# Weights moved behind the last V, the output weight in contiguous rows, and an earlier max, in a decode-attention kernel

## Chip, cores and metric

The kernel runs on one core of a Trainium2 chip. The metric is device microseconds (us) of one execution, the median of several runs; the span in a profile is about 1.8 us shorter than the time of the same run. Engines: PE is the matrix engine (PEld its weight loads), DVE the vector engine, ACT the scalar engine, SP the engine that issues the loads.

## The reference, cut to what matters

```python
xn  = layernorm(x)                                   # x: 1 x 1 x 640
q   = xn @ wq                                        # 640 -> 32 heads x 128
p   = softmax(q . k_cache * 128**-0.5)               # per head, 32768 keys; k, v: 8.39 MB a head each
o   = p @ v_cache
out = x + o.reshape(1, 1, 4096) @ wo                 # 4096 x 640
        + (silu(xn @ w_gate) * (xn @ w_up)) @ w_down # F = 1728
```

All tensors are bf16. Keys and values of 32 heads are 537 MB; wq and wo are 5.24 MB each, the three MLP weights 6.6 MB together.

## The kernel before

A ring of three slots of 64 KB per partition holds everything that is loaded. SP issues the loads in the order of `units`, each waiting until its slot is free. Here `H` is 32, `D` 640, `NJ` 256 (keys per partition), `NCD` 5, `FB` 14.

```python
units = [("wq",), ("ffn",)]
for h in range(H):
    units.append(("k", h))
    if h >= 1: units.append(("v", h - 1))
units += [("wo",), ("v", H - 1)]
slot = position in units % 3
TAIL = [128, 64, 32, 16, 16]      # the last V comes in five pieces, each with its own semaphore

# [cut] SP:
e.dma_start(wo, A_wo.rearrange("(h d) n -> d h n", d=DH))      # 128 partitions x 32 runs of 1280 B

# [cut] PE, one head: scores of h, then P @ V of h - 1
def head(h):
    scores(h)                     # after DVE multiplied K by q, PE folds 128 columns into 8 (L248, L267)
    if h >= 1:
        total(h - 1)
        pv_half(h - 1, 0)         # L279: 32 matmuls of 512 columns
    turn(h)                       # transposes the row maxima
    if h >= 1: pv_half(h - 1, 1)  # 32 more
    spread(h)                     # spreads the head's maximum; exp waits for it
    if h >= 2: fold(h - 2)        # o as a column

# [cut] PE, the end
fold(H - 2); wait wo
for h in range(H - 1): att(h)     # L358: 5 matmuls a head, weights wo_v[:, h, :, c] (every 5th column)
total(H - 1)
pv_last()                         # L292: 256 matmuls of one column, waiting for the five pieces
att(H - 1)                        # then DVE adds the residual, SP stores
```

The MLP is computed at the start, while the first keys are loaded.

Of the kernel before, what the change touches and what calls it, by code (L numbers as in the profile page):

```python
# [5 lines left out]
ALU = mybir.AluOpType  # L6
# [6 lines left out]
def bass_parallel_sum__gqa_block_cached__swiglu_ffn__decode_kernel(  # L13
# [33 lines left out]
    TAIL = [128, 64, 32, 16, 16]  # L47
    W = 512 // DH
    assert sum(TAIL) == NJ and NHF == 4 and (H - H0) % PER == 0 and PER % SLOTS == 0
    assert PER % PR == 0 and PER % SR == 0  # L50
    HA = 5
# [5 lines left out]
    units = [("wq",), ("ffn",)]  # L57
# [4 lines left out]
    units += [("wo",), ("v", H - 1)]  # L62
# [11 lines left out]
    with ExitStack() as es:  # L74
# [14 lines left out]
        ocol = sbt("ocol", [128, H], BF16)  # L89
        hcol = sbt("hcol", [128, FB], BF16)  # L90
# [15 lines left out]
        s_x, s_wq, s_wo, s_out = sem("x"), sem("wq"), sem("wo"), sem("o")  # L106
        s_ffn = sem("ffn")
# [9 lines left out]
        s_fpd, s_fx = sem("ffn_down"), sem("ffn_x")  # L117
        s_exp, s_pv, s_o4, s_fold, s_ov = sem("exp"), sem("pv"), sem("o4"), sem("fold"), sem("ov")
        s_f, s_fa, s_fd = sem("ffn_pe"), sem("ffn_act"), sem("ffn_dve")
        s_att, s_fin = sem("att"), sem("fin")  # L120
        block = es.enter_context(nc.Block())
# [23 lines left out]
        wo = flat[:, WO_S * CE:WO_S * CE + H * D].rearrange("p (h n) -> p h n", h=H)  # L145
        wo_v = wo.rearrange("p h (m c) -> p h m c", c=NCD)
        assert H * D <= CE
# [23 lines left out]
        with nc.psum_tensor("ps8", [128, 8, 512], F32) as ps8:  # L171
            bank = [ps8[:, b, :] for b in range(8)]
            O = ps8[0:W, 4, :]
            OL = ps8[:, 5, 0:1]
            acc = ps8[:, 6, 0:NCD]
            fold_ps = ps8[:, 6, 8:9]
            misc = ps8[:, 7, :]

            @block.sync
            def sp(e):  # L180
                owner = {}
                for u in units:
# [15 lines left out]
                    elif u[0] == "v":  # L198
                        e.dma_start(ring[:, s, :], kv_src(A_v_cache, u[1], 0, NJ)).then_inc(s_slot[s], 16)
                        owner[s] = (s_pv, u[1] + 1)  # L200
                    elif u[0] == "ffn":
                        e.dma_start(wg, B_w_gate.rearrange("(p c) n -> p (c n)", c=NCD)).then_inc(s_ffn, 16)
                        e.dma_start(wu, B_w_up.rearrange("(p c) n -> p (c n)", c=NCD)).then_inc(s_ffn, 16)
                        e.dma_start(flat[:, d0:d0 + FM * D], B_w_down[0:FM * 128, :].rearrange(  # L204
                            "(p j) n -> p (j n)", j=FM)).then_inc(s_ffn, 16)
                        e.dma_start(wd[0:FL, FM, :], B_w_down[FM * 128:F, :]).then_inc(s_ffn, 16)
                        owner[s] = (s_fpd, 1)
                    else:
                        e.dma_start(wo, A_wo.rearrange("(h d) n -> d h n", d=DH)).then_inc(s_wo, 16)
# [4 lines left out]
            @block.gpsimd  # L214
            def pool(g):
                for n, t in enumerate((ident, identf)):
                    g.memset(t[:, :], 0.0).then_inc(s_const, 1)
                    g.wait_ge(s_const, 2 * n + 1)
                    g.affine_select(out=t[:, :], in_=t[:, :], compare_op=ALU.not_equal, fill=1.0, base=0,
                                    pattern=[[-1, 128]], channel_multiplier=1).then_inc(s_const, 1)  # L220

            @block.tensor
            def pe(t):
# [48 lines left out]
                def pv_half(h, half):  # L272
                    s = slot_of[("v", h)]
                    if half == 0:
# [3 lines left out]
                    for j in range(half * NJ // 2, (half + 1) * NJ // 2, W):  # L278
                        mm = t.matmul(O, lhsT=P[:, h % PR, j:j + W], rhs=ring[:, s, j * DH:(j + W) * DH],  # L279
                                      start=(j == 0), stop=(j + W == NJ))  # L280
                    if half == 1:
                        mm.then_inc(s_pv, 1)

                def pv_last():
                    h = H - 1
                    s = slot_of[LASTV]
                    t.wait_ge(s_exp, H)
                    j = 0
                    for i, n in enumerate(TAIL):
                        t.wait_ge(s_tail[i], 16)  # L290
                        for _ in range(n):
# [3 lines left out]
                    mm.then_inc(s_pv, 1)  # L295
# [29 lines left out]
                def head(h):  # L325
                    scores(h)
                    if h >= 1:
                        total(h - 1)
                        pv_half(h - 1, 0)
                    turn(h)  # L330
                    if h >= 1:
                        pv_half(h - 1, 1)
                    spread(h)
                    if h >= 2:
# [3 lines left out]
                t.wait_ge(s_ffn, 64)  # L338
                for off, w in ((0, wg_v), (FB, wu_v)):
                    for j in range(FB):  # L340
                        n = 128 if j < FM else FL
                        for c in range(NCD):
                            mm = t.matmul(misc[0:n, off + j:off + j + 1], lhsT=hidden(w, c, j),  # L343
                                          rhs=xn[:, c:c + 1], start=(c == 0), stop=(c == NCD - 1))
                mm.then_inc(s_f, 1)
                first = True
                t.wait_ge(s_fd, 8)
                for j in range(FB):
                    n = 128 if j < FM else FL
                    for c in range(NCD):  # L350
                        mm = t.matmul(acc[:, c:c + 1], lhsT=wd_v[0:n, j, :, c], rhs=hcol[0:n, j:j + 1],
                                      start=first, stop=(j == FB - 1), skip_group_check=True)
                        first = False
                mm.then_inc(s_fpd, 1)

                def att(h):
                    for c in range(NCD):
                        mm = t.matmul(acc[:, c:c + 1], lhsT=wo_v[:, h, :, c], rhs=ocol[:, h:h + 1],  # L358
                                      start=(h == 0 and c == 0), stop=(h == H - 1), skip_group_check=True)
                    return mm  # L360

                t.wait_ge(s_fx, 1)
                for h in range(H0):
                    head(h)
                with t.Fori(0, (H - H0) // PER) as i:
# [3 lines left out]
                    group[0] = None  # L369
                fold(H - 2)  # L370
                t.wait_ge(s_wo, 16)
                t.wait_ge(s_ov, H)
                for h in range(H - 1):
                    att(h)
                total(H - 1)
                pv_last()
# [193 lines left out]
```

## Time and profile before

| | before |
|---|---|
| time | 1294.11 us, 3 runs, 1293.77 to 1294.47 |
| load queue, share of 16 engines | 99.5% |
| moved | 554 MB at 429 GB/s |
| PE / DVE / ACT busy | 80% / 52% / 4% |
| last load landed, end of span | 1285.7, 1292.1 us |

The page of the kernel before: engines' busy time, then in 40 slices of the span the busy share of the DMA engines in tenths and what they moved, then the load queue.

```profile
PE 1036.7 (80%) x5147; PEld 263.8 (20%) x3227; DVE 669.9 (52%) x407; ACT 51.9 (4%) x139; POOL 1.1 (0%) x8
...
DMA  9999999999999999999999999999999999999997
GB/s 400 449 424 427 443 425 435 436 434 428 436 434 438 428 436 438 426 434 438 426 434 438 430 432 436 434 432 432 438 434 428 436 438 426 434 438 428 432 401 315
...
q1 hardware_dynamic: 14704, 554.00, 99.5%
```

The DMA engines are full in every slice but the last. Whatever happens on PE and DVE inside the span is hidden unless it starves the queue; what is not hidden is what comes after the last byte has landed.

The chain that ended last shows the same: key loads hand over to each other at a fixed pace (start us, duration us, what).

```profile
184.33 41.80 DMA ring<-in_A_k_cache_dram
...
261.74 41.80 DMA ring<-in_A_k_cache_dram
```

The landings are at 226.1 and 303.5: 77.4 us for two heads, that is four loads of 8.39 MB, 433 GB/s.

The load of wo is the slow spot. First the issues of the last V but one and of wo, then their times from issue to landing (last column, us), then what moved between 1253 and 1262 us.

```profile
1214.95 0.33 SPq L199 DMA_DIRECT2D ring<-in_A_v_cache_dram  x1
1229.19 0.39 SPq L209 DMA_DIRECT2D ring<-in_A_wo_dram  x1
```
```profile
ring<-in_A_wo_dram SPq DMA_DIRECT2D x1, 5120.0 KB, 37.0
...
ring<-in_A_v_cache_dram SPq DMA_DIRECT2D x31, 36.8
```
```profile
DMA packets 2550, 3.26 MB, mean 363 GB/s; under 512 B 0, under 2 KB 2550, under 8 KB 2550
```

The 36.8 is the median of the 31 V loads; head 30's own is the same. V of head 30 landed at 1214.95 + 36.8 = 1251.8, wo at 1229.19 + 37.0 = 1266.2: 14.4 us for 5.24 MB, 363 GB/s, and every packet is under 2 KB.

The end of the kernel before (start us, duration us, engine, line, instruction, count, and in brackets the idle before it with what ended it):

```profile
1271.32 6.33 PE L358 MATMUL ps<-ocol,ring 128*128 128x1 bf16 x155 [0.36 <-ACT ocol L408]
...
1277.93 1.76 PE L292 MATMUL ps<-P,ring 128*128 128x1 bf16 x61
...
1279.93 3.55 PE L292 MATMUL ps<-P,ring 128*128 128x1 bf16 x128 [0.23 <-issue]
...
1285.86 1.92 PE L292 MATMUL ps<-P,ring 128*128 128x1 bf16 x67 [2.38 <-issue]
...
1287.82 0.22 DVE L538 TENSOR_SCALAR ocol<-ps,rzb 128x1 bf16<-128x1 f32 x1 [9.54 <-PE ps L292]
...
1288.10 0.36 PE L358 MATMUL ps<-ocol,ring 128*128 128x1 bf16 x5 [0.32 <-DVE ocol L538]
...
1288.69 0.35 SPq L211 DMA_DIRECT2D out_dram<-outb  x1
```

The last piece of V was issued at 1260.6 and took 25.1 us, so it landed at 1285.7. PE starts its last stretch at 1285.86, but with 67 matmuls to do, not only the 16 of the last piece: before it stands an idle time of 2.38 us called "issue", in which PE waited for nothing that the profile shows.

### The profile page before, as it was taken

Reading aid. Unit: us, or ns where it says so; the run is one execution under the profiler, and the core shown is the slowest. Engines: PE = TensorE matmul, PEld = TensorE weight load, DVE = VectorE, ACT = ScalarE, POOL = GpSimd, SP = SyncE. Lnnn points to the kernel's source line nnn. Section 1 sums busy time; section 2 is a strip of 40 time slices with the busy share of each in tenths; the row PEclk is TensorE's granted clock in tenths of the full one; section 3 lists DMA queues with packets and bytes.
Section 4 is the critical chain, followed back from the end, with each engine's and each line's share of the span. In section 5 each row is a group of like instructions: output and inputs, shape, how many; then the busy total and the mean of one; then the engine's idle time right before and its main releaser. Section 6 shows DMA issues by size and latency. Waiting matters only on the chain.

```text
span 1292.1 us, 9830 instructions
## 1 busy us (share of the span) xinstructions
PE 1036.7 (80%) x5147; PEld 263.8 (20%) x3227; DVE 669.9 (52%) x407; ACT 51.9 (4%) x139; POOL 1.1 (0%) x8
## 2 busy tenths in 40 slices
PE   3678879877779877778877778877778877778977
PEld 1301222111222111222111222111222111222115
DVE  0485444666444666444666444666444666444560
ACT  2000000000000000000000000000000000000000
POOL 0000000000000000000000000000000000000000
PEclk9588899888889888899888899888889888889886
DMA  9999999999999999999999999999999999999997
GB/s 400 449 424 427 443 425 435 436 434 428 436 434 438 428 436 438 426 434 438 426 434 438 430 432 436 434 432 432 438 434 428 436 438 426 434 438 428 432 401 315
DMA packets 14717, 554.16 MB, mean 429 GB/s; under 512 B 1329, under 2 KB 5490, under 8 KB 5746
## 3 DMA queue, kind: packets, MB, share of 16 engines
q1 hardware_dynamic: 14704, 554.00, 99.5%
q8 instruction: 9, 0.15, 0.0%
q14 instruction: 2, 0.02, 0.0%
q10 hardware_dynamic: 2, 0.00, 0.0%
HBM read 553.99 MB, written 0.00 MB: 429 GB/s over the span
## 4 chain that ended last, share of the span: by engine, by line
DMA 52%; PE 29%; DVE 12%; issue 6%; SPq 0%; DVEq 0%; ACT 0%
DMA ring<-in_A_k_cache_dram 52%; PE ps L279 17%; DVE ring L504 12%; PE ps L248 9%; PE ps L267 1%; PE ps L292 1%; PE ps L358 1%; PE ps L316 0%; PE ps L310 0%; PE ps L302 0%; DVEq L504 0%; SPq L204 0%; DVE sc L510 0%; PE ps L322 0%; ACT o L403 0%
## 5 line engine op out<-in xcount | busy, mean ns | idle before, releaser
L504 DVE TENSOR_TENSOR ring<-ring,qb 128x8192 bf16<-128x8192 bf16 x128 | 557.8, 4420 | 86.6 <-DMA ring<-in_A_k_cache_dram 86.5
L248 PE MATMUL ps<-ring,ident 128*128 128x512 bf16 x1920 | 496.0, 417 | 0.0
L279 PE MATMUL ps<-ring,P 128*4 128x512 bf16 x1984 | 438.3, 379 | 0.0
L267 PE MATMUL ps<-ring,ident 128*128 128x512 bf16 x128 | 56.1, 438 | 224.2 <-DVE ring L504 223.7
L279 PEld LDWEIGHTS ps<-ring,P 128*4 128x4 bf16 x1984 | 166.0, 85 | 245.4
L267 PEld LDWEIGHTS ps<-ring,ident 128*128 128x128 bf16 x128 | 12.6, 98 | 620.4 <-DVE ring L504 326.4
L522 DVE TENSOR_SCALAR negb<-ps 128x1 f32<-128x1 f32 x32 | 5.1, 158 | 215.5 <-PE ps L322 215.5
L510 DVE TENSOR_REDUCE sc<-ps 128x64 f32<-128x512 f32 x128 | 82.3, 684 | 62.6 <-PE ps L248 62.6
L519 DVE TENSOR_REDUCE m<-ps 1x1 f32<-1x128 f32 x32 | 8.9, 279 | 192.2 <-PE ps L316 192.2
L412 ACT ACTIVATE P<-sc,negb 128x256 bf16<-128x256 f32 x32 | 16.2, 508 | 1179.6 <-DVE negb L522 1179.6
L302 PE MATMUL ps<-identf,o 4*128 4x1 f32 x248 | 31.9, 245 | 0.9 <-ACT o L403 0.9
L310 PEld LDWEIGHTS ps<-rsum,ones 128*128 128x128 f32 x64 | 12.3, 194 | 99.0 <-issue 98.2
L302 PEld LDWEIGHTS ps<-identf,o 4*128 4x128 f32 x248 | 30.0, 187 | 0.9 <-ACT o L403 0.9
L403 ACT ACTIVATE o<-ps,rzb 4x512 f32<-4x512 f32 x31 | 21.0, 677 | 0.0
L240 PE MATMUL ps<-ring 128*128 128x512 bf16 x40 | 10.2, 420 | 11.2 <-DMA ring<-in_A_wq_dram 11.2
L473 DVE TENSOR_SCALAR sg<-sg 128x13 f32<-128x13 f32 (+1 forms) x2 | 0.2, 156 | 34.3 <-ACT sg L393 34.3
L516 DVE TENSOR_REDUCE pmax<-sc 128x1 f32<-128x256 f32 x32 | 13.4, 420 | 0.0
L343 PE MATMUL ps<-xn,ring 128*128 128x1 bf16 (+1 forms) x140 | 8.7, 198 | 5.7 <-DMA ring<-in_B_w_down_dram 5.7
L316 PE MATMUL ps<-identf,pmax 128*1 128x128 f32 x64 | 12.2, 272 | 1.2 <-DVE pmax L516 1.2
L322 PE MATMUL ps<-m,ones 1*128 1x1 f32 x64 | 12.1, 256 | 0.4 <-DVE m L519 0.4
L322 PEld LDWEIGHTS ps<-m,ones 1*128 1x128 f32 x64 | 9.4, 182 | 14.2 <-issue 13.5
L492 DVE RECIPROCAL rzb<-ps 128x1 f32<-128x1 f32 x32 | 5.0, 158 | 9.8 <-PE ps L310 9.8
(50 smaller groups left out, 88.2 us busy)
## 6 DMA issues: line engine op xcount, KB each, us to landing
ring<-in_A_wq_dram SPq DMA_DIRECT2D x1, 5120.0 KB, 15.3
ring<-in_A_wo_dram SPq DMA_DIRECT2D x1, 5120.0 KB, 37.0
ring<-in_A_v_cache_dram SPq DMA_DIRECT2D x1, 4096.0 KB, 22.2
ring<-in_B_w_gate_dram SPq DMA_DIRECT2D x1, 2160.0 KB, 19.9
ring<-in_B_w_up_dram SPq DMA_DIRECT2D x1, 2160.0 KB, 24.6
ring<-in_B_w_down_dram SPq DMA_DIRECT2D x1, 2080.0 KB, 28.6
ring<-in_A_v_cache_dram SPq DMA_DIRECT2D x1, 2048.0 KB, 21.6
ring<-in_A_v_cache_dram SPq DMA_DIRECT2D x1, 1024.0 KB, 23.6
```

What stands on the lines that cost most here:

```text
L248: return t.add_instruction(mybir.InstMatmult(start_tensor_calc=False, stop_tensor_calc=stop, tile_size=(128, 128), tile_position=(0, 0), l ...
L267: t.matmul(ob, lhsT=ident[:, :], rhs=src, start=True, stop=False)
L279: mm = t.matmul(O, lhsT=P[:, h % PR, j:j + W], rhs=ring[:, s, j * DH:(j + W) * DH], start=(j == 0), stop=(j + W == NJ))
L292: mm = t.matmul(OL, lhsT=ring[:, s, j * DH:(j + 1) * DH], rhs=P[:, h % PR, j:j + 1], start=(j == 0), stop=(j == NJ - 1))
L302: mm = t.matmul(fold_ps, lhsT=o4[:, m * DH:(m + 1) * DH], rhs=identf[0:W, m:m + 1], start=(m == 0), stop=(m == W - 1))
L322: t.matmul(misc[:, 128:129], lhsT=ones[0:1, :], rhs=m1[0:1, h % SR:h % SR + 1], start=True, stop=True).then_inc(s_b, 1)
L358: mm = t.matmul(acc[:, c:c + 1], lhsT=wo_v[:, h, :, c], rhs=ocol[:, h:h + 1], start=(h == 0 and c == 0), stop=(h == H - 1), skip_group_che ...
L403: a.activation(out=o4[:, :], in_=O, func=ACTF.Copy, scale=rzb[0:W, h % SR:h % SR + 1]).then_inc(s_o4, 1)
L412: a.activation(out=P[:, h % PR, :], in_=sc[:, :], func=ACTF.Exp, bias=negb[:, h % SR:h % SR + 1], scale=c_scale, accum_out=rsum[:, h % SR: ...
L504: v.tensor_tensor(out=kh, in0=kh, in1=q[:, None, :].to_broadcast([128, HF, DH]), op=ALU.mult).then_inc(s_mul, 1)
L510: v.tensor_reduce(out=sc[:, i * HF:(i + 1) * HF], in_=bank[i].rearrange("p (j e) -> p j e", e=G), axis=AX.X, op=ALU.add).then_inc(s_red, 1)
L516: v.tensor_reduce(out=pmax[:, h % SR:h % SR + 1], in_=sc[:, :], axis=AX.X, op=ALU.max).then_inc(s_max, 1)
```

## The change

Its intent: keep the stream of loads at full rate, and have as little as possible to do after the last byte. The weights of the MLP and of the output projection go behind the last V, wo last and in contiguous rows per partition, in pieces, so that only two rows' worth of projection (10 matmuls) follow the last landing. For that the head outputs must be laid out 32 consecutive elements per partition, which one matmul with a block mask does. In each head `turn` and `spread` move up by a quarter and a half of the PV.

```diff
-    TAIL = [128, 64, 32, 16, 16]
+    TAIL = [128, 64, 32, 32]
+    WTAIL = [16, 8, 4, 2, 2]
+    PARTS = [64, 64, 128]
-    units = [("wq",), ("ffn",)]
+    units = [("wq",)]
 ...
-    units += [("wo",), ("v", H - 1)]
+    units += [("v", H - 1), ("ffn",), ("wo",)]
 ...
-                        e.dma_start(wo, A_wo.rearrange("(h d) n -> d h n", d=DH)).then_inc(s_wo, 16)
+                        wo_src = A_wo.rearrange("(p j) n -> p (j n)", j=OC)
+                        for i, n in enumerate(WTAIL):          # [shortened]
+                            e.dma_start(wo[:, j * D:(j + n) * D], wo_src[:, j * D:(j + n) * D]).then_inc(s_wo[i], 16)
 ...
                     scores(h)
                     if h >= 1:
                         total(h - 1)
-                        pv_half(h - 1, 0)
+                        pv_part(h - 1, 0)
                     turn(h)
                     if h >= 1:
-                        pv_half(h - 1, 1)
+                        pv_part(h - 1, 1)
                     spread(h)
+                    if h >= 1:
+                        pv_part(h - 1, 2)
 ...                                                           # PE, the end
+                total(H - 1)
+                pv_last([0])
                 fold(H - 2)
-                t.wait_ge(s_wo, 16)
-                for h in range(H - 1):                         # [shortened]
-                    att(h)
-                total(H - 1)
-                pv_last()
-                att(H - 1).then_inc(s_att, 1)
+                pv_last(range(1, len(TAIL))).then_inc(s_pv, 1)
+                hidden_part(0)
+                t.matmul(op, lhsT=oblk[:, :, :], rhs=fold32[:, :], start=True, stop=True).then_inc(s_op, 1)
+                hidden_part(1).then_inc(s_f, 1)
+                down()
+                project().then_inc(s_att, 1)
 ...                                                           # DVE
+                v.tensor_tensor(out=oblk[:, :, :], in0=ocol[:, :, None].to_broadcast([128, H, RB]),
+                                in1=blk[:, None, :].to_broadcast([128, H, RB]), op=ALU.mult)
```

Cut: the constants on the pool engine, the semaphores, the bodies of the new functions, and the MLP's ACT and DVE steps, which move from the start to the end.

More of the change, by code (lines that the diff above doesn't have):

```diff
@@ L46, in bass_parallel_sum__gqa_block_cached__swiglu_ffn__decode_kernel @@
     SR = 3
-    TAIL = [128, 64, 32, 16, 16]
+    TAIL = [128, 64, 32, 32]
+    RB = DH // 32
+    OC = H * DH // 128
+    WTAIL = [16, 8, 4, 2, 2]
+    PARTS = [64, 64, 128]
     W = 512 // DH
-    assert sum(TAIL) == NJ and NHF == 4 and (H - H0) % PER == 0 and PER % SLOTS == 0
+    assert sum(TAIL) == NJ and sum(PARTS) == NJ and NHF == 4 and (H - H0) % PER == 0 and PER % SLOTS == 0
     assert PER % PR == 0 and PER % SR == 0
+    assert OC == 32 and H * RB == 128 and sum(WTAIL) == OC
     HA = 5
@@ L89, in bass_parallel_sum__gqa_block_cached__swiglu_ffn__decode_kernel @@
         ocol = sbt("ocol", [128, H], BF16)
+        oblk = sbt("oblk", [128, H, RB], BF16)
+        blk = sbt("blk", [128, RB], BF16)
+        fold32 = sbt("fold32", [128, OC], BF16)
+        ot = sbt("ot", [128, OC], BF16)
         hcol = sbt("hcol", [128, FB], BF16)
@@ L105, in bass_parallel_sum__gqa_block_cached__swiglu_ffn__decode_kernel @@
         s_slot = [sem(f"slot{i}") for i in range(SLOTS)]
-        s_x, s_wq, s_wo, s_out = sem("x"), sem("wq"), sem("wo"), sem("o")
-        s_ffn = sem("ffn")
+        s_x, s_wq, s_out = sem("x"), sem("wq"), sem("o")
+        s_wo = [sem(f"wo{i}") for i in range(len(WTAIL))]
+        s_ffn = [sem(n) for n in ("gate", "up", "down")]
         s_tail = [sem(f"tail{i}") for i in range(len(TAIL))]
@@ L116, in bass_parallel_sum__gqa_block_cached__swiglu_ffn__decode_kernel @@
         s_neg, s_z, s_rz = sem("neg"), sem("z"), sem("rz")
-        s_fpd, s_fx = sem("ffn_down"), sem("ffn_x")
         s_exp, s_pv, s_o4, s_fold, s_ov = sem("exp"), sem("pv"), sem("o4"), sem("fold"), sem("ov")
@@ L120, in bass_parallel_sum__gqa_block_cached__swiglu_ffn__decode_kernel @@
         s_att, s_fin = sem("att"), sem("fin")
+        s_ob, s_op, s_ot = sem("o_blocks"), sem("o_ps"), sem("o_rows")
         block = es.enter_context(nc.Block())
@@ L144, in hidden @@
             return w[:, c, FM * 128:F]
-        wo = flat[:, WO_S * CE:WO_S * CE + H * D].rearrange("p (h n) -> p h n", h=H)
-        wo_v = wo.rearrange("p h (m c) -> p h m c", c=NCD)
-        assert H * D <= CE
+        wo = flat[:, WO_S * CE:WO_S * CE + OC * D]
+        wo_v = wo.rearrange("p (j m c) -> p j m c", j=OC, c=NCD)
+        assert OC * D <= CE
         def kv_src(cache, h, j0, n):
@@ L174, in bass_parallel_sum__gqa_block_cached__swiglu_ffn__decode_kernel @@
             OL = ps8[:, 5, 0:1]
+            op = ps8[:, 5, 8:8 + OC]
             acc = ps8[:, 6, 0:NCD]
@@ L177, in bass_parallel_sum__gqa_block_cached__swiglu_ffn__decode_kernel @@
             misc = ps8[:, 7, :]
+            ffn = bank[0]
             @block.sync
@@ L201, in sp @@
                     elif u[0] == "ffn":
-                        e.dma_start(wg, B_w_gate.rearrange("(p c) n -> p (c n)", c=NCD)).then_inc(s_ffn, 16)
-                        e.dma_start(wu, B_w_up.rearrange("(p c) n -> p (c n)", c=NCD)).then_inc(s_ffn, 16)
+                        e.dma_start(wg, B_w_gate.rearrange("(p c) n -> p (c n)", c=NCD)).then_inc(s_ffn[0], 16)
+                        e.dma_start(wu, B_w_up.rearrange("(p c) n -> p (c n)", c=NCD)).then_inc(s_ffn[1], 16)
                         e.dma_start(flat[:, d0:d0 + FM * D], B_w_down[0:FM * 128, :].rearrange(
-                            "(p j) n -> p (j n)", j=FM)).then_inc(s_ffn, 16)
-                        e.dma_start(wd[0:FL, FM, :], B_w_down[FM * 128:F, :]).then_inc(s_ffn, 16)
-                        owner[s] = (s_fpd, 1)
-                    else:
-                        e.dma_start(wo, A_wo.rearrange("(h d) n -> d h n", d=DH)).then_inc(s_wo, 16)
+                            "(p j) n -> p (j n)", j=FM)).then_inc(s_ffn[2], 16)
+                        e.dma_start(wd[0:FL, FM, :], B_w_down[FM * 128:F, :]).then_inc(s_ffn[2], 16)
+                    else:
+                        wo_src = A_wo.rearrange("(p j) n -> p (j n)", j=OC)
+                        j = 0
+                        for i, n in enumerate(WTAIL):
+                            e.dma_start(wo[:, j * D:(j + n) * D], wo_src[:, j * D:(j + n) * D]).then_inc(s_wo[i], 16)
+                            j += n
                 e.wait_ge(s_fin, 1)
@@ L215, in pool, with done @@
             def pool(g):
-                for n, t in enumerate((ident, identf)):
-                    g.memset(t[:, :], 0.0).then_inc(s_const, 1)
-                    g.wait_ge(s_const, 2 * n + 1)
-                    g.affine_select(out=t[:, :], in_=t[:, :], compare_op=ALU.not_equal, fill=1.0, base=0,
-                                    pattern=[[-1, 128]], channel_multiplier=1).then_inc(s_const, 1)
+                n = [0]
+                def done(ins):
+                    ins.then_inc(s_const, 1)
+                    n[0] += 1
+                    g.wait_ge(s_const, n[0])
+                for t in (ident, identf):
+                    done(g.memset(t[:, :], 0.0))
+                    done(g.affine_select(out=t[:, :], in_=t[:, :], compare_op=ALU.not_equal, fill=1.0, base=0,
+                                         pattern=[[-1, 128]], channel_multiplier=1))
+                done(g.memset(blk[:, :], 0.0))
+                for a in range(RB):
+                    done(g.tensor_copy(out=fold32[a * 32:(a + 1) * 32, :],
+                                       in_=ident[a * 32:(a + 1) * 32, a * 32:a * 32 + OC]))
+                for a in range(RB):
+                    done(g.memset(blk[a * 32:(a + 1) * 32, a:a + 1], 1.0))
+                assert n[0] == 5 + 2 * RB
             @block.tensor
@@ L270, in scores, with pv_part @@
                         mm.then_inc(s_qk, 1)
-                def pv_half(h, half):
+                def pv_part(h, part):
                     s = slot_of[("v", h)]
-                    if half == 0:
+                    if part == 0:
                         wait(s_exp, h, lambda h: h + 1)
@@ L277, in pv_half, with pv_last @@
                         wait(s_slot[s], h, lambda h: 16 * use_of[("v", h)])
-                    for j in range(half * NJ // 2, (half + 1) * NJ // 2, W):
+                    first = sum(PARTS[:part])
+                    for j in range(first, first + PARTS[part], W):
                         mm = t.matmul(O, lhsT=P[:, h % PR, j:j + W], rhs=ring[:, s, j * DH:(j + W) * DH],
                                       start=(j == 0), stop=(j + W == NJ))
-                    if half == 1:
+                    if part == len(PARTS) - 1:
                         mm.then_inc(s_pv, 1)
-                def pv_last():
+                def pv_last(pieces):
                     h = H - 1
                     s = slot_of[LASTV]
-                    t.wait_ge(s_exp, H)
-                    j = 0
-                    for i, n in enumerate(TAIL):
+                    for i in pieces:
                         t.wait_ge(s_tail[i], 16)
-                        for _ in range(n):
+                        j = sum(TAIL[:i])
+                        for _ in range(TAIL[i]):
                             mm = t.matmul(OL, lhsT=ring[:, s, j * DH:(j + 1) * DH], rhs=P[:, h % PR, j:j + 1],
@@ L294, in pv_last @@
                             j += 1
-                    mm.then_inc(s_pv, 1)
+                    return mm
                 def fold(h):
@@ L328, in head, with hidden_part @@
                         total(h - 1)
-                        pv_half(h - 1, 0)
+                        pv_part(h - 1, 0)
                     turn(h)
                     if h >= 1:
-                        pv_half(h - 1, 1)
+                        pv_part(h - 1, 1)
                     spread(h)
+                    if h >= 1:
+                        pv_part(h - 1, 2)
                     if h >= 2:
                         fold(h - 2)
-                t.wait_ge(s_ffn, 64)
-                for off, w in ((0, wg_v), (FB, wu_v)):
+                def hidden_part(i):
+                    t.wait_ge(s_ffn[i], 16)
+                    w = (wg_v, wu_v)[i]
                     for j in range(FB):
@@ L342, in pe, with down, project @@
                         for c in range(NCD):
-                            mm = t.matmul(misc[0:n, off + j:off + j + 1], lhsT=hidden(w, c, j),
+                            mm = t.matmul(ffn[0:n, i * FB + j:i * FB + j + 1], lhsT=hidden(w, c, j),
                                           rhs=xn[:, c:c + 1], start=(c == 0), stop=(c == NCD - 1))
-                mm.then_inc(s_f, 1)
-                first = True
-                t.wait_ge(s_fd, 8)
-                for j in range(FB):
-                    n = 128 if j < FM else FL
-                    for c in range(NCD):
-                        mm = t.matmul(acc[:, c:c + 1], lhsT=wd_v[0:n, j, :, c], rhs=hcol[0:n, j:j + 1],
-                                      start=first, stop=(j == FB - 1), skip_group_check=True)
-                        first = False
-                mm.then_inc(s_fpd, 1)
-                def att(h):
-                    for c in range(NCD):
-                        mm = t.matmul(acc[:, c:c + 1], lhsT=wo_v[:, h, :, c], rhs=ocol[:, h:h + 1],
-                                      start=(h == 0 and c == 0), stop=(h == H - 1), skip_group_check=True)
-                    return mm
-                t.wait_ge(s_fx, 1)
+                    return mm
+                def down():
+                    t.wait_ge(s_ffn[2], 32)
+                    t.wait_ge(s_fd, 8)
+                    first = True
+                    for j in range(FB):
+                        n = 128 if j < FM else FL
+                        for c in range(NCD):
+                            t.matmul(acc[:, c:c + 1], lhsT=wd_v[0:n, j, :, c], rhs=hcol[0:n, j:j + 1],
+                                     start=first, stop=False, skip_group_check=True)
+                            first = False
+                def project():
+                    j = 0
+                    for i, n in enumerate(WTAIL):
+                        t.wait_ge(s_wo[i], 16)
+                        for _ in range(n):
+                            for c in range(NCD):
+                                mm = t.matmul(acc[:, c:c + 1], lhsT=wo_v[:, j, :, c], rhs=ot[:, j:j + 1],
+                                              start=False, stop=(j == OC - 1), skip_group_check=True)
+                            j += 1
+                    return mm
                 for h in range(H0):
@@ L369, in pe @@
                     group[0] = None
+                total(H - 1)
+                pv_last([0])
                 fold(H - 2)
-                t.wait_ge(s_wo, 16)
-                t.wait_ge(s_ov, H)
-                for h in range(H - 1):
-                    att(h)
-                total(H - 1)
-                pv_last()
-                t.wait_ge(s_ov, H + 1)
-                att(H - 1).then_inc(s_att, 1)
+                pv_last(range(1, len(TAIL))).then_inc(s_pv, 1)
+                hidden_part(0)
+                t.wait_ge(s_const, 5 + 2 * RB)
+                t.wait_ge(s_ob, 1)
+                t.matmul(op, lhsT=oblk[:, :, :], rhs=fold32[:, :], start=True, stop=True).then_inc(s_op, 1)
+                hidden_part(1).then_inc(s_f, 1)
+                down()
+                t.wait_ge(s_ot, 1)
+                project().then_inc(s_att, 1)
             @block.scalar
@@ L388, in act @@
                     a.activation(out=qb[:, b * 512:(b + 1) * 512], in_=bank[b], func=ACTF.Copy).then_inc(s_qc, 1)
-                a.wait_ge(s_f, 1)
-                a.activation(out=sg[:, 0, 0:FB - 1], in_=misc[:, 0:FB - 1], func=ACTF.Exp,
-                             scale=-1.0).then_inc(s_fa, 1)
-                a.activation(out=sg[0:FL, 0, FB - 1:FB], in_=misc[0:FL, FB - 1:FB], func=ACTF.Exp,
-                             scale=-1.0).then_inc(s_fa, 1)
                 group, wait = counter(a, HA)
@@ L432, in act @@
                 column(H - 2)
+                a.wait_ge(s_op, 1)
+                a.activation(out=ot[:, :], in_=op, func=ACTF.Copy).then_inc(s_ot, 1)
+                a.wait_ge(s_f, 1)
+                a.activation(out=sg[:, 0, 0:FB - 1], in_=ffn[:, 0:FB - 1], func=ACTF.Exp,
+                             scale=-1.0).then_inc(s_fa, 1)
+                a.activation(out=sg[0:FL, 0, FB - 1:FB], in_=ffn[0:FL, FB - 1:FB], func=ACTF.Exp,
+                             scale=-1.0).then_inc(s_fa, 1)
             @block.vector
@@ L463, in dve @@
                 assert n_a[0] == 11
-                v.wait_ge(s_fa, 2)
-                pieces = [(slice(0, 128), slice(0, FM)), (slice(0, FL), slice(FM, FB))]
-                n = 0
-                for stage in range(4):
-                    for p, f in pieces:
-                        fu = slice(FB + f.start, FB + f.stop)
-                        if stage == 0:
-                            ins = v.tensor_scalar(out=sg[p, 0, f], in0=sg[p, 0, f], scalar1=1.0, scalar2=None,
-                                                  op0=ALU.add)
-                        elif stage == 1:
-                            ins = v.reciprocal(out=sg[p, 1, f], in_=sg[p, 0, f])
-                        elif stage == 2:
-                            ins = v.tensor_tensor(out=sg[p, 0, f], in0=sg[p, 1, f], in1=misc[p, f], op=ALU.mult)
-                        else:
-                            ins = v.tensor_tensor(out=hcol[p, f], in0=sg[p, 0, f], in1=misc[p, fu], op=ALU.mult)
-                        ins.then_inc(s_fd, 1)
-                        n += 1
-                    v.wait_ge(s_fd, n)
-                v.wait_ge(s_fpd, 1)
-                v.tensor_tensor(out=xf[:, :], in0=xf[:, :], in1=acc, op=ALU.add).then_inc(s_fx, 1)
                 group, wait = counter(v, H0)
@@ L539, in dve @@
                                 scalar2=None, op0=ALU.mult).then_inc(s_ov, 1)
+                v.wait_ge(s_const, 5 + 2 * RB)
+                v.wait_ge(s_ov, H + 1)
+                v.tensor_tensor(out=oblk[:, :, :], in0=ocol[:, :, None].to_broadcast([128, H, RB]),
+                                in1=blk[:, None, :].to_broadcast([128, H, RB]), op=ALU.mult).then_inc(s_ob, 1)
+                v.wait_ge(s_fa, 2)
+                pieces = [(slice(0, 128), slice(0, FM)), (slice(0, FL), slice(FM, FB))]
+                n = 0
+                for stage in range(4):
+                    for p, f in pieces:
+                        fu = slice(FB + f.start, FB + f.stop)
+                        if stage == 0:
+                            ins = v.tensor_scalar(out=sg[p, 0, f], in0=sg[p, 0, f], scalar1=1.0, scalar2=None,
+                                                  op0=ALU.add)
+                        elif stage == 1:
+                            ins = v.reciprocal(out=sg[p, 1, f], in_=sg[p, 0, f])
+                        elif stage == 2:
+                            ins = v.tensor_tensor(out=sg[p, 0, f], in0=sg[p, 1, f], in1=ffn[p, f], op=ALU.mult)
+                        else:
+                            ins = v.tensor_tensor(out=hcol[p, f], in0=sg[p, 0, f], in1=ffn[p, fu], op=ALU.mult)
+                        ins.then_inc(s_fd, 1)
+                        n += 1
+                    v.wait_ge(s_fd, n)
                 v.wait_ge(s_att, 1)
```

## The prediction

> **What bounds the kernel now: the DMA engines, throughout.** The table of DMA queues gives the load queue 99.5% of 16 engines' span: 554 MB at a mean of 429 GB/s. The chain of waits shows keys landing every 77.4 us per two heads, four loads of 8.39 MB, so 433 GB/s; this agrees with the fabric ceiling of 435 GB/s in the Trainium skill, "DMA: Bandwidth & Descriptors", section "Where 436 GB/s comes from". PE is busy 80%, DVE 52%; the queue is fed some 14 to 25 us ahead.
>
> **Not touched.** The bytes are the same. Max and spread ahead of half the PV release the exp about 7 us sooner (32 matmuls of PV take 7.0 us in the chain), but under the stream: no gain in 32 heads. The MLP's weights take 15.8 us of the stream (wq landed at 16.0, the last w_down at 31.9), wherever they stand.
>
> **Removed.**
> 1. The output weight comes in 1280-byte runs. By issues and landings, V of head 30 landed at 1251.75 and wo at 1266.2: 14.45 us for 5.24 MB, 363 GB/s. In contiguous rows at 430 GB/s: 12.2 us. Gain 2.2 us. The page's section "Specifications" names 512 B as the least for line rate; this trace disagrees.
> 2. The tail. The last V piece landed at 1285.7, the span ended at 1292.1: 6.4 us. In the timeline PE starts again at 1285.86 with 67 matmuls (1.92 us; it had lost 2.38 us to "issue", probably an instruction fetch, so more than the last piece's 16 were left), then scaling 0.22, five matmuls 0.36, sum 0.16, store about 3.4. After, only 10 projection matmuls, sum and store follow the last landing: about 4.3 us. Gain 2.1 us.
>
> **Added, and does it fit?** 27.5 us of weights land behind the last V. Estimates from the trace's durations, in after's time, landings up to V30 being 15.9 us sooner: K31 at 1216.5, its scores done 1237.7, V31 landed 1255.3, gate 1260.5, up 1265.6, down 1271.2, wo half 1277.3, all 1283.5. PE: PV of 30 to 1252.2, folds and last PV (256 x 27.7 ns) to 1262, gate (70 x 62 ns) to 1266.3, transposing matmul 0.4, up to 1271.1, exp and eight DVE operations 1.5, down 3.05 to 1275.7, projection 160 x 40.8 ns = 6.5 us. So PE reaches wo 1.6 us before its first piece and the stream stays the limit, but thinly: two stalls of 2.4 us would show. Pool constants and the block multiply are hidden[...].
>
> **On the critical path:** 4.3 us, less 0 to 1.5 for stalls. 1294.1 - 4.0 = **1290.1 us**, range **1287.9 to 1292.3**. Faster by over 2%: 1%; within 2%: 98%; slower by over 2%: 1%.
>
> **What would show it.** First key about 16 us sooner (near 36, not 51.9); no drop to 363 GB/s near the end; last landing near 1283.5, 4 to 4.7 us before the end of the span; still 77.4 us per two heads; PE idle about 1.6 us before the projection's first piece.
>
> **What would make it wrong.** PE late at the end (wo landed before PE reached it, idle put down to issue): 2 to 4 us lost, no gain left. Small pieces of wo landing unevenly. A gap in the stream near the start, since V0 now waits for the q projection and K2 for K0's scores (I expect both issued over 15 us early).

## The result

| | before | after |
|---|---|---|
| time, median us | 1293.94 (4 runs, 1293.46 to 1294.47) | 1289.89 (4 runs, 1289.61 to 1290.10) |
| ratio, 95% interval | | 0.9968 (0.9951 to 0.9986) |
| span of the profiled run | 1292.1 | 1288.2 |
| last load landed | 1285.7 | 1283.9 |
| from there to the end of the span | 6.4 | 4.3 |
| of this, until the store is issued | 2.95 | 0.90 |

A ratio is the mean time of one kernel's runs over that of the other's of the same rounds, so not quite the ratio of the medians. Executions over 1.5% slower than the fastest of the same kernel are left out of the means. The gain is 4.0 us, and the time lies inside the predicted range. The interval leaves 1 out, so the gain is real; it is far below 2%.

The page after, the same lines:

```profile
DMA  9999999999999999999999999999999999999998
GB/s 421 426 425 446 426 429 442 429 431 440 431 431 433 435 431 429 440 431 431 440 427 431 444 427 431 442 429 431 435 433 433 429 438 433 427 442 431 427 422 340
...
q1 hardware_dynamic: 11168, 554.00, 99.6%
```

The stream is as full as before. The chain shows the same pace, with landings at 984.3 and 1061.7, again 77.4 us for two heads:

```profile
942.90 41.40 DMA ring<-in_A_k_cache_dram
...
1020.22 41.48 DMA ring<-in_A_k_cache_dram
```

The first key lands 16.6 us sooner (35.3 instead of 51.9) because the MLP no longer stands before it, but that is not a gain: the MLP's 16 us stand at the other end.

The last piece of wo (SP line L223), its issue and its landing, 1254.2 + 29.7 = 1283.9:

```profile
L223 SPq DMA_DIRECT2D ring<-in_A_wo_dram x1: 444/444/444, 1254.2 to 1254.2; - x1
...
DMA to landing us min/median/max: 29.7/29.7/29.7
```

By the same kind of lines the last MLP piece (issued at 1239.1, 32.5 us to its landing) was in at 1271.6, so wo took 12.3 us of the stream instead of 14.4.

The end after, in the same form:

```profile
1258.41 1.33 PE L320 MATMUL ps<-P,ring 128*128 128x1 bf16 x44
...
1260.45 2.40 PE L320 MATMUL ps<-P,ring 128*128 128x1 bf16 x84 [0.70 <-issue]
...
1262.70 2.79 PE L374 MATMUL ps<-xn,ring 128*128 128x1 bf16 x44
...
1266.92 1.77 PE L374 MATMUL ps<-xn,ring 128*128 128x1 bf16 x26 [1.43 <-issue]
...
1268.67 4.39 PE L374 MATMUL ps<-xn,ring 128*128 128x1 bf16 x70
...
1274.55 3.02 PE L385 MATMUL ps<-hcol,ring 128*128 128x1 bf16 x70 [1.49 <-DVE hcol L576]
...
1277.78 6.76 PE L395 MATMUL ps<-ot,ring 128*128 128x1 bf16 x160 [0.21 <-DMA ring<-in_A_wo_dram]
...
1284.84 0.35 SPq L226 DMA_DIRECT2D out_dram<-outb  x1
```

Here L320 is the last PV, L374 the hidden layer, L385 the down matmul, L395 the projection. After the last landing at 1283.9 there is only a rest of the projection, the sum and the store. But PE did not wait for wo as it should: it reached the first piece 0.21 us before it could start and then ran 160 matmuls without a gap, and twice before it had stood idle for "issue", 0.70 and 1.43 us.

### The profile page after: what moved, and what is told of

Same layout as the page of the kernel before. It is cut to its first block, busy times and chain, and to the rows that moved or that the text cites. A ratio compares the mean times of both kernels' runs of the same rounds, so it can differ in the third digit from the quotient of the medians.

```text
span 1288.2 us, 9847 instructions
## 1 busy us (share of the span) xinstructions
PE 1043.7 (81%) x5148; PEld 263.9 (20%) x3228; DVE 670.0 (52%) x407; ACT 52.2 (4%) x140; POOL 2.5 (0%) x17
## 4 chain that ended last, share of the span: by engine, by line
DMA 53%; PE 31%; DVE 11%; issue 6%; DVEq 0%; SPq 0%
DMA ring<-in_A_k_cache_dram 51%; PE ps L308 17%; PE ps L276 11%; DVE ring L522 10%; DMA ring<-in_A_wo_dram 2%; PE ps L295 1%; PE ps L395 1%; PE ps L350 0%; PE ps L344 0%; PE ps L338 0%; DVEq L522 0%; DVE sc L528 0%; DVE pmax L534 0%; SPq L199 0%; DVEq L172 0%
## 5 line engine op out<-in xcount | busy, mean ns | idle before, releaser
L308 PE MATMUL ps<-ring,P 128*4 128x512 bf16 x1984 | 443.3, 379 | 0.0
L308 PEld LDWEIGHTS ps<-ring,P 128*4 128x4 bf16 x1984 | 163.4, 85 | 237.8
L540 DVE TENSOR_SCALAR negb<-ps 128x1 f32<-128x1 f32 x32 | 5.1, 158 | 108.4 <-PE ps L350 108.4
L446 ACT ACTIVATE P<-sc,negb 128x256 bf16<-128x256 f32 x32 | 16.2, 508 | 956.7 <-DVE negb L540 956.7
L442 ACT ACTIVATE ocol<-ps 128x1 f32 (+1 forms) x31 | 5.4, 174 | 222.1 <-PE ps L330 222.1
L344 PE MATMUL ps<-identf,pmax 128*1 128x128 f32 x64 | 12.2, 273 | 1.2 <-DVE pmax L534 1.2
L374 PE MATMUL ps<-xn,ring 128*128 128x1 bf16 (+1 forms) x140 | 8.9, 198 | 1.4 <-issue 1.4
```

Source lines behind the costliest of these rows:

```text
L308: mm = t.matmul(O, lhsT=P[:, h % PR, j:j + W], rhs=ring[:, s, j * DH:(j + W) * DH], start=(j == 0), stop=(j + W == NJ))
L344: t.matmul(misc[0:1, 0:128], lhsT=pmax[:, h % SR:h % SR + 1], rhs=identf[:, :], start=True, stop=True).then_inc(s_t, 1)
L446: a.activation(out=P[:, h % PR, :], in_=sc[:, :], func=ACTF.Exp, bias=negb[:, h % SR:h % SR + 1], scale=c_scale, accum_out=rsum[:, h % SR: ...
```

## The experiments

My theory: 2 us come from the run length of wo, 2 us from the shorter end, nothing from the early max and nothing from the place of the MLP. Rivals: the early max speeds each head, or the order of the stream is what counts. In the table, "landed" is the last load's landing and "rest" is from there to the end of the span, both of the profiled run. The kernel before took 1293.79, 1294.01 and 1293.78 us (medians of 9 runs) on the chips of the first four, the next four and the last run, so a difference of 0.2 us between runs of different chips says nothing.

| run | time, us (runs) | ratio to before (95%) | span | landed | rest |
|---|---|---|---|---|---|
| before | 1293.94 (4) | 1 | 1292.1 | 1285.7 | 6.4 |
| after | 1289.89 (4) | 0.9968 (0.9951 to 0.9986) | 1288.2 | 1283.9 | 4.3 |
| e1 short runs | 1291.31 (5) | 0.9981 (0.9967 to 0.9995) | 1289.5 | 1285.6 | 3.9 |
| e2 max back | 1289.70 (5) | 0.9968 (0.9955 to 0.9982) | 1287.9 | 1283.8 | 4.1 |
| e3 max alone | 1293.75 (5) | 1.0000 (0.9986 to 1.0013) | 1292.1 | 1285.9 | 6.2 |
| e4 MLP first | 1292.06 (5) | 0.9986 (0.9973 to 1.0000) | 1290.2 | 1283.6 | 6.6 |
| e5 MLP before last V | 1290.98 (5) | 0.9976 (0.9962 to 0.9989) | 1289.4 | 1283.9 | 5.5 |
| e6 packed columns | 1289.76 (5) | 0.9967 (0.9953 to 0.9980) | 1287.7 | 1284.0 | 3.7 |
| e7 after, shifted | 1290.54 (1) | | 1288.7 | 1283.8 | 4.9 |
| e8 rows, old place | 1297.93 (4) | 1.0031 (1.0015 to 1.0046) | 1296.0 | 1283.8 | 12.2 |
| e9 before, shifted | 1293.93 (5) | 1.0000 (0.9987 to 1.0014) | 1292.1 | 1285.7 | 6.4 |

All intervals are wider than the spread of the runs suggests: the ranges of e1 (1291.12 to 1291.90), e4 (1291.97 to 1292.12) and after (1289.61 to 1290.10) don't overlap.

### e1: the short runs put back

```diff
-wo_src = A_wo.rearrange("(p j) n -> p (j n)", j=OC)
+wo_src = A_wo.rearrange("(h d) n -> d h n", d=DH)      # pieces of 16, 8, 4, 2, 2 heads
-project(): rhs=ot[:, j:j + 1]
+project(): rhs=ocol[:, j:j + 1]                        # no transposing of the head outputs
```

> The changed kernel with one part undone: the output weight again in 1280-byte runs (pieces of 16, 8, 4, 2, 2 heads), still last in the stream, no transposing of the head outputs. My theory (2.2 us of the gain is run length, 2.1 us is the shorter tail): wo takes about 14.4 us of the stream again instead of 12.3, 1292.0 us, half the gain left. Rival (the gain comes from the order of the stream or from the early max, run length costs nothing): 1289.9 us, wo still 12.3 us.

Measured: 1291.31 us, 1.4 us of the gain lost. The last MLP load landed at 1271.6 as in the kernel after, the last of wo at 1285.6 instead of 1283.9. So wo took 14.0 us of the stream instead of 12.3, and the run length is worth about 1.7 us. The DMA engines were not short of work: from 1272 to 1282 they moved 363 GB/s and were as busy (1.07 in the view by windows) as in the kernel before from 1253 to 1262. (The order of the addresses changes with the run length; no run separates the two.) PE here waits for the last piece:

```profile
1282.36 3.05 PE L396 MATMUL ps<-ocol,ring 128*128 128x1 bf16 x70 [0.24 <-DMA ring<-in_A_wo_dram]
...
1285.67 0.56 PE L396 MATMUL ps<-ocol,ring 128*128 128x1 bf16 x10 [0.26 <-DMA ring<-in_A_wo_dram]
```

In both kernels the store is issued 0.9 us after the last landing. That the span moved by less than the landing comes from the store's own time to landing in the two profiled runs, 2.6 us here and 3.0 in the kernel after. So my theory holds with about 1.7 us where I expected 2.1, and the rival that run length costs nothing falls.

### e2 and e3: the early max, taken away and alone

```diff
 # e2, in the kernel after                     # e3, in the kernel before
-PARTS = [64, 64, 128]                         +PARTS = [64, 64, 128]
+PARTS = [128, 128]                             scores, part 0, turn, part 1, spread, part 2
```

> The changed kernel with max and spread put back behind the PV halves. My theory: the waits lie under the stream in all heads but the last; there the exp of the last head comes about 7 us later, just as its total is wanted, so 0 to 0.5 us slower, 1290.0 to 1290.4 us. Rival (the early max carries a good part of the gain, some 0.1 us a head or more): 1292 us or more.

> The kernel before with only max and spread moved ahead of half of the PV. My theory: no change, ratio 1.000 within 0.0003 (1293.9 us). Rival (the early max speeds each head): 1292 us or less.

Measured: e2 1289.70 us against 1289.89 for after, with overlapping ranges, where I had expected 0 to 0.5 us slower; e3 1293.75 us against 1293.79, ratio 1.0000. The early max is worth nothing in either kernel. The rival falls. The exp of a head does come sooner (in the list of groups, DVE's idle before the step that follows `spread` falls from 215.5 us in the kernel before to 108.4 in the kernel after), but only an idle engine has less idle time.

### e4: the MLP back at the start

```diff
-units = [("wq",)]
+units = [("wq",), ("ffn",)]
-units += [("v", H - 1), ("ffn",), ("wo",)]
+units += [("v", H - 1), ("wo",)]
 # hidden layer, silu and down again before the first head
```

> The changed kernel with the MLP's weights and arithmetic back at the start; only the output weight stays behind the last V, in contiguous rows. My theory (the place of the MLP in the stream is worth nothing; PE was 0.2 us late at the end of the changed kernel because the MLP stood before its projection): 1289.5 to 1289.9 us, PE idle 3 us or more before the first piece of wo. Rival (part of the gain is the first key landing 16 us sooner, or the MLP hiding at the end): 1291 us or more.

Measured: 1292.06 us. My theory fails here: the last load lands at 1283.6, as early as in the kernel after, yet the rest is 6.6 us. The timeline says why:

```profile
1261.17 7.07 PE L310 MATMUL ps<-ring,P 128*4 128x512 bf16 x32
...
1269.39 3.48 PE L322 MATMUL ps<-P,ring 128*128 128x1 bf16 x128
...
1274.58 2.53 PE L322 MATMUL ps<-P,ring 128*128 128x1 bf16 x89
...
1277.63 1.20 PE L322 MATMUL ps<-P,ring 128*128 128x1 bf16 x39 [0.51 <-issue]
...
1280.11 6.80 PE L398 MATMUL ps<-ot,ring 128*128 128x1 bf16 x160 [0.29 <-ACT ot L478]
```

PE is still in the PV of head 30 (L310) until 1268.2 and in the last PV (L322) until 1278.8; the transposing and its handovers take until 1280.11, and then 6.8 us of projection follow, 2.7 us after the first piece of wo was there (1277.4). The MLP's place is free for the stream but not for PE: behind the last V, its 16 us of loads are time in which PE works off its backlog, against some 12 us of matmuls that it adds (8.9 in the hidden layer, 3.0 in down). The rival was right about the size, but not for its first reason, the sooner first key: the landings are alike.

### e5: the MLP between the last two V

```diff
-units += [("v", H - 1), ("ffn",), ("wo",)]
+units += [("ffn",), ("v", H - 1), ("wo",)]
 # PE: total, hidden layer, last PV piece 0, down, the other pieces, transposing, projection
```

> The changed kernel with the MLP's weights between the V of head 30 and the last V, its matmuls ahead of the last PV; wo last as in the change. My theory, mended by the run with the MLP first (there PE was still busy with V30 and V31 when wo landed, and ended 2.3 us later): what the MLP's place does is to give PE time; here PE does the MLP while the last V streams, so the projection waits for its pieces (idle over 2 us before the first) and the span ends about 4.0 us after the last landing instead of 4.3: 1289.4 to 1289.7 us. Rival (the MLP must stand behind the last V): 1291 us or more.

Measured: 1290.98 us, 1.1 us slower than after and at the rival's end of the scale. I expected PE to have time; it had none.

```profile
1267.56 1.38 PE L385 MATMUL ps<-hcol,ring 128*128 128x1 bf16 x31
1270.54 1.77 PE L385 MATMUL ps<-hcol,ring 128*128 128x1 bf16 x39 [1.60 <-issue]
...
1272.24 2.53 PE L320 MATMUL ps<-P,ring 128*128 128x1 bf16 x89
1277.01 1.18 PE L320 MATMUL ps<-P,ring 128*128 128x1 bf16 x39 [2.24 <-issue]
...
1279.53 6.56 PE L395 MATMUL ps<-ot,ring 128*128 128x1 bf16 x160 [0.29 <-ACT ot L473]
```

The work is the same, but the two idles for "issue" are 1.60 and 2.24 us here, and the way from the last PV to the transposed outputs (1278.2 to 1279.5) lies open, where the kernel after covers it with half of the MLP. In both kernels the two idles end 6.47 us apart. In the kernel after, 44 slow matmuls of the hidden layer fill more of this time, so less of it is idle, 1.43 us instead of 2.24 (e7 and e9 show what these idles are). The projection starts 1.75 us later than in the kernel after.

### e6: adjacent columns, wrong on purpose

```diff
-wo_v = wo.rearrange("p (j m c) -> p j m c", j=OC, c=NCD)
+wo_v = wo.rearrange("p (j c m) -> p j m c", j=OC, c=NCD)
-wd_v = wd.rearrange("p j (m c) -> p j m c", c=NCD)
+wd_v = wd.rearrange("p j (c m) -> p j m c", c=NCD)
```

> Wrong result on purpose (columns of the output permuted): the changed kernel with the weights of down and projection read as 128 adjacent columns rather than every fifth. If the step between columns is what makes a projection matmul 42 ns instead of the 27.7 ns of the last PV, the projection's 160 take about 4.5 us of PE instead of 6.8, PE waits for the last pieces, and the end moves to 4.0 us after the last landing: 1289.5 us. Rival (the 42 ns are the pace of PE at its lower clock for any such pair): still 42 ns and 1289.9 us.

Its output is permuted. Measured: 1289.76 us, rest 3.7 us. A projection matmul takes 28 ns (80 in 2.27 us) instead of 42, so the step of five columns is what costs, and PE now waits for the pieces:

```profile
1277.86 2.27 PE L395 MATMUL ps<-ot,ring 128*128 128x1 bf16 x80 [0.95 <-DMA ring<-in_A_wo_dram]
...
1280.87 0.35 PE L395 MATMUL ps<-ot,ring 128*128 128x1 bf16 x7 [0.73 <-DMA ring<-in_A_wo_dram]
...
1284.02 0.43 PE L395 MATMUL ps<-ot,ring 128*128 128x1 bf16 x10 [0.35 <-DMA ring<-in_A_wo_dram]
```

The time hardly moves (0.13 us, with overlapping ranges): the lateness of PE at the end of the kernel after costs about 0.1 us. From the last landing to the store's issue it took 0.90 us in the kernel after and 0.78 here (0.91 in e1, where PE waits too). The rest of the difference in "rest" is the store's own landing, 3.0 us against 2.5. There is no version with a clear gain behind this.

### e7 and e9: what the idle called "issue" is

Both kernels with 20 more tiny matmuls at their very start, 40 instructions, no change in the result.

```diff
+for _ in range(5):
     for c in range(NCD):
         mm = t.matmul(misc[:, 8 + c:9 + c], lhsT=xrow_v[:, :, c], rhs=one1[:, :], start=True, stop=True)
```

> The changed kernel with 20 more tiny matmuls (40 instructions) at its very start, the result the same. Theory: the idle put down to issue in the tail (0.70 and 1.43 us, 128 matmuls or 256 instructions apart) is the refill of the instruction buffer in blocks of 256; then the first gap comes 24 matmuls into the second part of the last PV instead of 44, and the second 24 matmuls into the gate half instead of 44. Rival (the gaps are waits for data, the last pieces of V or the gate weights): both stay at 44. The time about the same, 1290 us.

Measured, e7: the gaps come after 24 matmuls instead of 44, both of them.

```profile
1258.19 0.80 PE L321 MATMUL ps<-P,ring 128*128 128x1 bf16 x24
...
1260.47 2.93 PE L321 MATMUL ps<-P,ring 128*128 128x1 bf16 x104 [1.47 <-issue]
...
1263.26 1.58 PE L375 MATMUL ps<-xn,ring 128*128 128x1 bf16 x24
...
1266.68 2.99 PE L375 MATMUL ps<-xn,ring 128*128 128x1 bf16 x46 [1.84 <-issue]
...
1281.77 3.84 PE L396 MATMUL ps<-ot,ring 128*128 128x1 bf16 x93 [0.45 <-issue]
```

So the idle hangs on the position in the program, not on data, and the two gaps stay 128 matmuls, that is 256 instructions, apart. The Trainium skill, page "Runtime: NRT & Kernel Launch", section "Instruction fetch mechanics", says that instructions are refilled in blocks of 16 KiB, 256 instructions, and that the cost of a boundary is mostly hidden. The trace agrees on the 256 and not on the hiding. The gaps end at 1260.47 and 1266.68, where those of the kernel after ended at 1260.45 and 1266.92: shifted in the program, but hardly in time. A third gap of 0.45 us opened inside the projection, and this single run took 1290.54 us (its state is called unknown, as there is only one). Its store was issued 2.1 us after the last landing, against 0.9 in the kernel after: where the gaps fall in the program decides whether PE is done in time.

> The kernel before with the same 20 tiny matmuls added at its start. The run that shifted the changed kernel moved the gaps to 24 matmuls, as the instruction-refill theory had it, and left their ends within 0.3 us of where they were. Theory A (the refill of a block of 256 instructions is paced by itself, about 6 us a block while the load queue is full): the gap now comes 20 matmuls sooner in the last PV and PE resumes at about the same time with some 87 matmuls left instead of 67, 0.2 to 0.6 us slower, 1294.2 to 1294.6 us. Theory B (a stall of fixed length at the boundary): the gap ends 0.5 us sooner or falls into a wait for data, the same time or up to 1.2 us faster. Theory C (the idle is a wait for the third piece of V): gap unmoved, still 67 matmuls left, 1294.0 us.

Measured, e9: 1293.93 us against 1293.78.

```profile
1277.86 1.23 PE L293 MATMUL ps<-P,ring 128*128 128x1 bf16 x41
...
1279.25 3.55 PE L293 MATMUL ps<-P,ring 128*128 128x1 bf16 x128 [0.16 <-issue]
...
1285.46 2.46 PE L293 MATMUL ps<-P,ring 128*128 128x1 bf16 x87 [2.66 <-issue]
```

The gap moved by 20 matmuls as theories A and B have it, and C falls. It is longer (2.66 us instead of 2.38) and 87 matmuls are left instead of 67, as A says; PE resumes 0.4 us sooner, though, and the time rises by 0.15 us, inside the noise and just under what I had written for A. That the refill has a pace of its own, about 6 us a block here (1279.25 to 1285.46), fits best: from one gap's end to the next, one block later, it is 5.9 us in the kernel before and 6.5 in the kernel after and in e5. Why it has this pace is not settled.

That it is a refill, the shifts alone only suggest; the traces show it. The view of the DMA queues lists packets of 0.02 MB on a queue called "instruction", their size in the packed trace 16,384 bytes. The kernel before from 1283.5 to 1284 us, e9 from 1282 to 1283, and the kernel after from 1264.25 to 1264.5:

```profile
q8 instruction: 1, 0.02, 13.3%
...
q8 instruction: 1, 0.02, 6.7%
...
q8 instruction: 1, 0.02, 26.8%
```

These packets start at 1283.53, 1282.91 and 1264.40, and PE resumes 2.33, 2.55 and 2.52 us later. Read in this way, each of the 21 idles for "issue" at the end of these kernels (all but e8 have some) ends 2.3 to 2.7 us after such a packet has started. In the kernel before PE had run through its matmuls at 1283.48, before the packet had even started.

### e8: contiguous rows at the old place

```diff
-units += [("v", H - 1), ("wo",)]       # from e4
+units += [("wo",), ("v", H - 1)]
```

> The kernel of the run with the MLP first, with wo in contiguous rows back at its place before the last V (as in the kernel before), so that the whole projection comes after the last V. It measures the run length alone at the old place: from the landing of V30 to that of wo 12.3 us if my figure of 2.2 us is right, about 12.8 if it is the 1.6 us that the run with the 1280-byte runs at the end showed. The tail pays for the whole projection: about 1297 us, slower than before.

Measured: wo landed at 1264.3, V of head 30 at 1251.9, 12.4 us against 14.4 in the kernel before; the last load at 1283.8 against 1285.7. So at the old place too the run length is worth about 2 us. The time is 1297.93 us: in contiguous rows nothing of the projection can start before all heads are done, and 160 matmuls (6.56 us) and the transposing follow the last V. The layout that helps the stream hurts the end, unless wo comes last.

## Why the prediction was right

- **The bound.** Right: the stream stays full, 77.4 us for two heads in both kernels, and all of the gain is at the last loads and behind them.
- **Run length, 2.2 us.** The mechanism was right and the size a little high: 1.7 us in e1, 1.9 to 2.0 us in e8.
- **The end, 2.1 us.** Right in the sum, 6.4 to 4.3. In the kernel before some 1.4 us of the 6.4 (an estimate: 51 matmuls of 27.7 ns, 67 less the last piece's 16) were there because of the instruction refill. So by this estimate most of the 2.1 us is a stall that no longer falls behind the last landing, and the smaller part is work that no longer stands there. The prediction named the refill as probable and counted its 67 matmuls; e7, e9 and the instruction packets show it.
- **The early max, no gain.** Right, by e2 and e3.
- **"The MLP's weights take 15.8 us of the stream, wherever they stand."** Right for the stream (16.2 us at the end). I read too much into it later, when I expected e4 to cost nothing: the place of the MLP decides whether PE is done in time, and is worth 2.2 us here.
- **"PE reaches wo 1.6 us before its first piece."** Wrong: 0.21 us. The step left the refill out of the sum of PE's work and only named it as a risk, with 0 to 1.5 us off the gain; it took 0.70 + 1.43 = 2.1 us. The stream and PE end almost together, and this cost about 0.1 us. That it cost no more is in part luck: nobody chose where the refills fall, and in the single run of e7, with 20 more matmuls at the start, PE was done over 1 us later.

The two main terms, 1.8 for the stream and 2.1 for the end, give the 3.9 us by which the span fell. The parts of the change don't add up singly: contiguous rows at the old place are 4 us slower than before (e8), with wo last 1.7 us faster (e4), with the MLP behind the last V too 4 us faster (after).

## What to carry to other kernels

When the loads are full from start to end, only two things count: the rate of the slowest load, and what is left to do after the last byte; order the last loads so that the compute backlog shrinks while they stream. A layout that is better for the loads can force work behind the last load, so move order and layout together and measure them together. In the sum of an engine's work at the end, count its instructions too: 256 of them here cost up to 2.7 us of idle when they were used up faster than they came, and the packets of the instruction queue in the DMA view show when they come.

## What the Trainium skill lacked or had wrong

- Page "DMA: Bandwidth & Descriptors", section "Specifications", gives 512 B as the least transfer for line rate. Runs of 1280 B took 14.0 and 14.4 us for 5.24 MB (363 GB/s in the DMA view), contiguous rows 12.3 and 12.4 us.
- Page "Runtime: NRT & Kernel Launch", section "Instruction fetch mechanics", calls the cost of a 16 KiB block boundary mostly hidden. With the load queue full and matmuls of 28 to 62 ns, PE stood idle for up to 2.66 us at such boundaries, and the page gives no time for the refill under load (PE resumed 2.3 to 2.7 us after the start of its packet, and 5.9 to 6.5 us passed from one gap's end to the next, one block later).
- Page "TensorE: Matmul & The Clock Gate", section "Weight-path perf modes — Fast Weight Load (FWL) and DoubleRow", allows weights that are packed or strided and gives no cost of the step; what other pages say of steps in SBUF has no time for a weight load. Here a load of 128 weights and a one-column matmul took 28 ns with adjacent columns and 42 ns with every fifth (e6), and 62 ns with every thirteenth in the hidden layer, where no run tests whether the step is the cause.
